# Start-up filler on a zeroed tile, one norm moved ahead of the next tile's first sums, and two column-tiled products made neighbours, in a fused linear-attention and FFN block

## The chip, the cores and the metric

The kernel runs on one core of one Trainium2 chip. The metric is device time in microseconds (us) of one execution; lower is better. The engines are TensorE (PE in the profile, with PEld for its weight loads), VectorE (DVE), ScalarE (ACT), GpSimd (POOL) and SyncE (SP), which issues most loads. A profile gives times from the first instruction of the span, and the measured time was 1.4 to 1.5 us longer than the span (225.25 against 223.8 in the profiled execution of the kernel before). The pitch is the time from the start of one matmul to the start of the next. In profile lines psT is the memory (PSUM) that matmul results go to.

## The reference

```python
x  = A_x                                   # 1 x 2048 x 640, bf16
xn = layernorm(x)                          # over 640 features
q, k, v = split(xn @ wqkv)                 # 32 heads of 20
phi(t)  = where(t > 0, t + 1, exp(t)) + 1e-6
kv  = einsum(phi(k), v);  z = sum_s phi(k) # per head
o   = (phi(q) @ kv) / (phi(q) . z + 1e-6)
s   = o @ wo
g   = silu(relu(xn @ w1) @ w2)             # w1: 640 x 1728, w2: 1728 x 640
out = x + s * g
```

The 1728 columns of w1 are 13 chunks of 128 and a half chunk of 64.

## The kernel before

Tokens are handled in 16 tiles of 128. For each tile VectorE takes the sums of two halves (`bn_stats`), aggregates them (`bn_aggr`) and normalises; GpSimd computes the inverse root of the variance (for tile 0 ScalarE and VectorE do). The step that normalises tile 1 is called norm 1, and so on. The normalised tile is transposed (for the first four tiles on TensorE, against an identity) and multiplied with the weights. The program gives each engine a list of operations with waits on semaphores, and the traces show the lists worked in order: in e7 below VectorE stands still for 1.00 us ahead of norm 1, for most of it with the next entry, tile 2's sums, ready (tile 2 landed at 6.14, norm 1 started at 6.88). These are the parts that the change touches:

```python
sc.op("POOL", lambda eng: eng.memset(ident[:], 0.0), ...)
sc.op("POOL", lambda eng: eng.affine_select(out=ident[:], ...), ...)        # L357
...
def warm(n):                                 # filler: keeps TensorE busy
    sc.group("PE", [(lambda eng: eng.matmul(ps[7][:, 0:P], lhsT=ident[:], rhs=ident[:], ...))
                    for _ in range(n)], R=[("ident",)], W=[("ps", 7)])      # L367
warm(33)
...
def LN_root_pool(t):                         # GpSimd: add eps (L391), then pow -0.5 (L393)
    ...
x_load(0); x_load(1); w_load(<first 3/5 of the key weights>)                # cut
x_load(2); x_load(3); w_load(<last 2/5 of the key weights>)                 # cut
...
LN_norm(0, late_loads)
transposes(0, 4)
warm(11)
xnT_copy(0, 4)
LN_stat(1, 1)
LN_aggr(1)
LN_root_pool(1)
LN_stat(2, 0)          # first sums of tile 2: wait for its load
LN_norm(1)             # waits for GpSimd's root of tile 1
K_mm(0, 0, range(0, KS))
transposes(1, 5)
...
def H_half(jp):        # half chunk of w1: 64 output columns, two token chunks side by side (L530)
    ...
def den():             # attention denominator: 32 output columns, four side by side (L616)
    ...
    # in the last token chunk: ... H_block(3,4), den(), H_block(3,5) ... H_block(3,12)
for jp in range(2):
    lastW1 = H_half(jp)
# then the sums over tokens, G = xn^T . phi(k) (L711)
```

## Time and profile before

| what | value |
|---|---|
| time, median of the first 3 executions | 225.07 us (224.62 to 225.43) |
| TensorE busy | 217.5 of 223.8 us |
| filler starts | 1.59 us |
| tile 2 landed | 7.08 us |
| transposes of tile 2 start | 10.10 us |
| steps between tilings in the stretch 99 to 113 us | 4 of 93 to 105 ns each |

The landing times in this document are the last of the 16 completion records of a load in the trace. First the page of the kernel before: part 1, and the engines' shares of the chain of part 4.

```profile
PE 217.5 (97%) x1447; PEld 134.8 (60%) x1457; DVE 102.8 (46%) x191; ACT 88.4 (39%) x146; POOL 45.2 (20%) x63
...
PE 94%; DMA 2%; DVE 2%; SPq 1%; issue 1%
```

TensorE fills the span, but the chain has 6% that is not TensorE, and it lies at the start and the end. The next lines are the chain that ended last, in order of time (start, length, what), of the kernel before.

```profile
2.20 4.89 DMA reg<-in_A_x_dram
7.08 0.02 issue
7.11 0.49 DVE stats L383
7.60 0.35 DVE reg L412
7.95 0.41 DVE stats L383
8.36 0.02 issue
8.38 0.21 DVE mv L387
8.59 0.76 DVE stats L383 x2
...
9.60 0.46 DVE reg L412
10.06 0.05 issue
10.10 0.45 PE psT L422 x5
```

The load that ends at 7.08 is tile 2. VectorE takes its first sums, then normalises tile 1 (L412 at 7.60; the chain counts a piece from the end of the one before it, its own start is 7.52), and so on to norm 2 and the transposes of tile 2 at 10.10. From there on it is TensorE, almost without a break, to the end. So the start is a chain of a load and VectorE.

The timeline of TensorE around the two tiled products of the kernel before (start, length from the first start to the last end, engine, line; idle time and its cause in brackets):

```profile
97.74 2.32 PE L517 MATMUL psT<-reg 128*128 128x512 bf16 x10
99.99 1.26 PE L616 MATMUL psT<-pqT,zmat 128*32 128x512 bf16 x20
101.41 8.58 PE L517 MATMUL psT<-reg 128*128 128x512 bf16 x39 [0.16 <-issue]
109.92 2.35 PE L530 MATMUL psT<-reg 128*64 128x512 bf16 x20
112.20 0.99 PE L711 MATMUL psT<-reg 128*128 128x320 bf16 x6
```

The weights' form (128\*128, 128\*32, 128\*64) shows the changes of tiling. The single records behind these lines give the steps: the last full-width start before 99.99 is at 99.68, 309 ns where neighbours are 216 apart. The 0.16 us before 101.41 is not idle time: that line has 39 matmul records and 40 weight loads, so the record of the first matmul is missing.

### The profile page before, as it was taken

How to read it: one execution, taken by the hardware profiler on the slowest of the kernel's cores; microseconds unless marked ns; L12 is line 12 of the kernel's file. 1: busy time of each engine (PE TensorE's matmuls, PEld its weight loads, DVE VectorE, ACT ScalarE, POOL GpSimd, SP SyncE). 2: the span in 40 equal slices, each digit the busy share in tenths (PEclk: the TensorE clock that was granted, in tenths of full speed). 3: DMA queues.
4: the chain of work that ended last, by engine and by line, in shares of the span. 5: the costliest groups of instructions: out<-in, count | busy, mean ns of one | idle time of the engine just before them, and what ended most of it. 6: DMA issues, size and time to landing. Idle time of an engine off the chain costs nothing.

```text
span 223.8 us, 3490 instructions
## 1 busy us (share of the span) xinstructions
PE 217.5 (97%) x1447; PEld 134.8 (60%) x1457; DVE 102.8 (46%) x191; ACT 88.4 (39%) x146; POOL 45.2 (20%) x63
## 2 busy tenths in 40 slices
PE   7999999999999999999999999999999999999993
PEld 6664555455554555444467778677767767776772
DVE  4669961796639772867000003940404041331472
ACT  4596966657665666654521111441021102102101
POOL 2426942322542245700000005000000000000001
PEclk9999999999999999999999999999999999999999
DMA  6999630012501150000899999900101010101030
GB/s 181 327 390 280 128 122 0 0 31 59 32 1 27 32 56 5 0 0 3 195 222 291 341 350 245 326 16 3 42 17 62 0 60 3 59 0 62 24 122 29
DMA packets 24333, 23.18 MB, mean 104 GB/s; under 512 B 9006, under 2 KB 23678, under 8 KB 24318
## 3 DMA queue, kind: packets, MB, share of 16 engines
q1 hardware_dynamic: 24174, 22.88, 37.2%
q8 instruction: 11, 0.18, 0.3%
q10 hardware_dynamic: 144, 0.08, 0.1%
q14 instruction: 4, 0.03, 0.0%
HBM read 15.75 MB, written 5.24 MB: 94 GB/s over the span
## 4 chain that ended last, share of the span: by engine, by line
PE 94%; DMA 2%; DVE 2%; SPq 1%; issue 1%
PE psT L778 26%; PE psT L517 25%; PE psT L711 10%; PE psT L494 10%; PE psT L439 9%; PE psT L817 8%; DMA reg<-in_A_x_dram 2%; PE psT L802 1%; PE psT L739 1%; PE psT L756 1%; PE psT L530 1%; DVE stats L383 1%; PE psT L724 1%; PE psT L616 1%; SPq L334 0%
## 5 line engine op out<-in xcount | busy, mean ns | idle before, releaser
L778 PE MATMUL psT<-reg,hT 128*128 128x320 bf16 x416 | 58.7, 299 | 0.3
L517 PE MATMUL psT<-reg 128*128 128x512 bf16 x252 | 56.8, 379 | 0.5 <-issue 0.2
L778 PEld LDWEIGHTS psT<-reg,hT 128*128 128x128 bf16 x416 | 40.3, 98 | 17.0 <-PE psT L756 1.6
L517 PEld LDWEIGHTS psT<-reg 128*128 128x128 bf16 x260 | 25.3, 98 | 29.2 <-ACT hT L521 0.4
L521 ACT ACTIVATE hT<-psT 128x512 bf16<-128x512 f32 x52 | 30.8, 600 | 17.7 <-PE psT L517 17.4
L774 ACT ACTIVATE reg<-psT 128x640 bf16<-128x640 f32 x16 | 10.8, 702 | 63.1 <-PE psT L778 34.8
L831 DVE TENSOR_TENSOR reg<-psT,reg 128x640 bf16<-128x640 f32 x14 | 11.5, 824 | 46.0 <-PE psT L817 46.0
L451 POOL TENSOR_TENSOR zacc<-zacc,reg 128x640 f32<-128x640 f32 x16 | 22.6, 1411 | 20.7 <-DVE reg L470 20.5
L439 PE MATMUL psT<-reg 128*128 128x320 bf16 x160 | 24.5, 299 | 0.0
L494 PE MATMUL psT<-reg 128*128 128x512 bf16 x98 | 21.8, 379 | 0.1
L711 PE MATMUL psT<-reg 128*128 128x320 bf16 x160 | 21.9, 299 | 0.0
L439 PEld LDWEIGHTS psT<-reg 128*128 128x128 bf16 x160 | 15.4, 98 | 7.8
L817 PE MATMUL psT<-reg,pqT 128*128 128x320 bf16 x140 | 20.0, 299 | 0.0
L711 PEld LDWEIGHTS psT<-reg 128*128 128x128 bf16 x160 | 15.6, 98 | 6.4 <-issue 0.4
L807 POOL TENSOR_TENSOR reg<-reg 128x320 bf16<-128x320 bf16 x1 | 0.8, 789 | 82.9 <-DVE reg L805 82.9
L817 PEld LDWEIGHTS psT<-reg,pqT 128*128 128x128 bf16 x140 | 13.7, 98 | 5.3
L727 DVE TENSOR_TENSOR reg<-psT,mh 120x120 bf16<-120x120 f32 (+1 forms) x6 | 1.5, 268 | 32.7 <-PE psT L724 32.6
L494 PEld LDWEIGHTS psT<-reg 128*128 128x128 bf16 x100 | 9.8, 98 | 11.1
L383 DVE BATCH_NORM_STATS2 stats<-reg 128x6 f32<-128x320 bf16 x32 | 14.2, 479 | 4.3 <-DMA reg<-in_A_x_dram 4.3
L501 ACT ACTIVATE er<-psT 128x512 bf16<-128x512 f32 x20 | 12.3, 614 | 9.1 <-PE psT L494 3.5
L456 ACT ACTIVATE ek<-psT 128x640 bf16<-128x640 f32 x16 | 11.4, 710 | 8.5 <-PE psT L439 8.4
L468 DVE TENSOR_SCALAR ek<-ek 128x640 bf16<-128x640 bf16 x16 | 6.1, 381 | 17.2 <-ACT ek L456 17.2
(63 smaller groups left out, 162.7 us busy)
## 6 DMA issues: line engine op xcount, KB each, us to landing
reg<-in_A_x_dram SPq DMA_DIRECT2D x16, 160.0 KB, 5.5
rden_by_feature<-rden SPq DMA_DIRECT2D x4, 640.0 KB, 8.8
reg<-rden_by_feature SPq DMA_DIRECT2D x5, 512.0 KB, 11.0
reg<-in_A_x_dram SPq DMA_DIRECT2D x4, 640.0 KB, 10.1
reg<-in_B_w_dram SPq DMA_DIRECT2D x2, 1120.0 KB, 10.1
out_dram<-reg SPq DMA_DIRECT2D x14, 160.0 KB, 1.8
reg<-in_B_w_dram SPq DMA_DIRECT2D x1, 1040.0 KB, 10.0
reg<-in_B_w_dram SPq DMA_DIRECT2D x1, 960.0 KB, 14.8
```

Source lines behind the costliest of these rows:

```text
L383: sc.op("DVE", lambda eng: eng.bn_stats(stats[:, t, a, :], xin[:, t % XR, HN * a:HN * (a + 1)]), R=[("xin", t % XR)], W=[("stats", t, a)])
L439: fns.append(lambda eng, a=a, k=k: eng.matmul(ps[b + a][:, 0:HN], lhsT=xnT[:, k, tok(t)], rhs=wqk[:, k, D + HN * a:D + HN * (a + 1)], star ...
L451: sc.op("POOL", lambda eng: eng.tensor_tensor(out=zacc[:, :], in0=zacc[:, :], in1=pk[:, t, :], op=ALU.add), R=[("zacc",), ("pk", t)], W=[( ...
L456: sc.op("ACT", lambda eng: eng.activation(out=e_.rearrange("p (a n) -> p a n", a=2), in_=ps2(b, HN), func=ACTF.Exp), R=[("ps", b), ("ps", ...
L494: sc.group("PE", [(lambda eng, k=k: eng.matmul(ps[b], lhsT=wqk[:, k, P * f:P * (f + 1)], rhs=xnT[:, k, schunk(j)], start=(k == 0), stop=(k ...
L501: sc.op("ACT", lambda eng: eng.activation(out=e_, in_=ps[b], func=ACTF.Exp), R=[("ps", b)], W=[("er_e", es)])
L517: a = sc.group("PE", [(lambda eng, k=k: eng.matmul(ps[b], lhsT=w1_sb[:, k, P * f:P * (f + 1)], rhs=xnT[:, k, schunk(j)], start=(k == 0), s ...
L521: sc.op("ACT", lambda eng: eng.activation(out=hT[:, f, schunk(j)], in_=ps[b], func=ACTF.Relu), R=[("ps", b)], W=[("hT", j, f)])
L711: fns.append(lambda eng, t=t, a=a: eng.matmul(ps[b + a][:, 0:HN], lhsT=xn[:, t, P * k:P * (k + 1)], rhs=pk[:, t, HN * a:HN * (a + 1)], sta ...
L778: fns = [(lambda eng, u=u, t=t, f=f, n=n: eng.matmul(ps[bs[n] + u][:, 0:HN], lhsT=hT[:, f, tok(t)], rhs=w2_sb[:, f, HN * n:HN * (n + 1)], ...
L817: sc.group("PE", [(lambda eng, c=c, a=a: eng.matmul(ps[b + a][:, 0:HN], lhsT=pqT[:, c, tok(t)], rhs=wf[:, c, HN * a:HN * (a + 1)], start=( ...
L831: sc.op("DVE", lambda eng: eng.tensor_tensor(out=tmpo[:, os_, lo:hi].rearrange(shp, a=na), in0=src, in1=g_sb[:, t, lo:hi].rearrange(shp, a ...
```

## The change

It makes three edits. The filler matmuls read a tile that VectorE zeroes, so they need not wait for GpSimd's identity; 38 in place of 33 keep their end where it was (near 5.1 us, starting from an estimated 1.05 in place of 1.59), at the slow pitch of 107 ns. Norm 1 goes ahead of the first sums of tile 2. The half-chunk products go directly behind the denominator product, so that the tiling changes three times in place of four (93 to 105 ns each in the kernel before).

```diff
+    fill = zmat[:, :, :].rearrange("p c h -> p (c h)")[:, 0:P]
+    sc.op("DVE", lambda eng: eng.memset(fill, 0.0), W=[("zmat",)])
+
     def warm(n):
-        sc.group("PE", [(lambda eng: eng.matmul(ps[7][:, 0:P], lhsT=ident[:], rhs=ident[:], start=True, stop=True))
-                        for _ in range(n)], R=[("ident",)], W=[("ps", 7)])
-    warm(33)
+        sc.group("PE", [(lambda eng: eng.matmul(ps[7][:, 0:P], lhsT=fill, rhs=fill, start=True, stop=True))
+                        for _ in range(n)], R=[("zmat",)], W=[("ps", 7)])
+    warm(38)
...
     LN_root_pool(1)
+    LN_norm(1)
     LN_stat(2, 0)
-    LN_norm(1)
...
                 if n == 9:
                     den()
+                    H_half(0)
+                    H_half(1)
...
-    for jp in range(2):
-        lastW1 = H_half(jp)
```

## The prediction

> **What bounds it now.** TensorE: busy 217.5 of 223.8 us (page, part 1), 94% of the chain that ended last; from 10.1 us the chain is TensorE nearly without a break. Before, it is the load of token tile 2 (landed 7.08), then VectorE (sums of tile 2 7.11, norm 1 7.52, sums 7.95, aggregation 8.38, sums of tile 3 8.59, norm 2 9.60), then the transposes of tile 2 at 10.10. A change earns only what it takes from that VectorE chain or from TensorE after 10.1.
>
> **1. Filler on a zeroed tile.** In the timeline the 33 fillers start at 1.59, released by GpSimd after the identity (memset 0.80, select 1.24 to 1.53). First work of engines starts at 0.80 and the identity's memset took 0.20, so I estimate the new start at 1.05. At the cold pitch (107 ns) 38 fillers end near 5.1, as 33 did: ahead of the first transposes (5.36, released by norm 0). VectorE idles until 3.16: its memset is free. What is bought is an earlier full clock: before, the pitch falls from 107 to 56 ns near 6.76. [...] If before 5.36, five transposes save 5 x 51 ns, but off the chain: tile 2 lands at 7.08 whatever TensorE does. Worth 0 to 0.3 us, 0.05 on average.
>
> **2. Norm 1 first.** Before, the sums of tile 2 waited for the load until 7.11 and norm 1 came behind, though its inverse root was ready at 6.92 (GpSimd, 6.35 + 0.57). After: norm 1 at 6.95, sums at 7.32 and 7.73, aggregation at 8.24 instead of 8.38. Norm 1 is 0.56 us earlier, but the chain gains only the idle time before 7.11: 0.14 us.
>
> **3. Products together.** In narrow timelines the last 128-column matmul starts at 99.68 and the den product at 99.99: 309 ns against the usual 216. The step back costs about the same (the "issue 0.16" after den is mostly a missing record: that line has 252 matmuls and 260 weight loads). The half-chunks pay 309 ns going in (109.61 to 109.92) and 312 going out (111.89 to 112.20). [...] the trace shows 93 to 100 ns each, four times. After: full to 32 columns, 32 to 64, 64 to full, so three[...]: 0.10 us gained[...]. All on the chain. PSUM banks: six in the ring, ScalarE evicts in 0.60 us while a block takes 1.08; no new wait. Gated loads still start behind the last up-projection product.
>
> **Sum.** 0.14 + 0.10 + 0.05 = 0.3 us of 225.07: 224.8 us, range 224.2 to 225.3. Run-to-run spread (0.8 us) exceeds the gain. Faster by over 2%: 0.01; within 2%: 0.98; slower: 0.01.
>
> **Right or wrong in the profile.** Filler start near 1.05; norm 1 near 6.95; transposes of tile 2 near 9.96; three steps of about 95 ns around 100 to 103 us and none at 112; span near 223.5.
>
> **What would make it wrong.** [...] tile 2 landing before 6.9, so that norm 1 delays its sums; GpSimd's root later than the load; a wait for a PSUM bank behind the half-chunks.

Passages that rest on something other than the traces of this case are cut out of the record, here and in one expectation (e4), and the cuts are marked. 0.14 (step 2) + 0.10 (step 3) + 0.05 (step 1) is 0.29, put as 0.3 us, which takes 225.07 to 224.8. In step 3 the alternative is 0.19 us if the step from 32 to 64 columns should cost nothing; it was not in the sum.

## The result, and the profile after

| | executions | median | range |
|---|---|---|---|
| before | 6 | 224.88 us | 224.62 to 225.43 |
| changed | 6 | 224.89 us | 224.84 to 224.95, and one of 465.64 |

The ratio of the fast executions is 0.9997 (95% interval 0.9983 to 1.0011). A ratio is the mean time of one kernel's fast runs over that of the other's of the same rounds, so it is not quite the ratio of the medians.

One execution, the profiled one, took 465.64 us. It is slow (over 1.5% above the fastest of the same kernel), and nothing below compares it with fast ones; a section of its own says what its trace shows. The profile of the changed kernel at the usual clock is that of its third run (e7 below; 223.4 us span). Its code has three lines more, so L383 of before is L386 here, L412 is L415, L616 is L619, L530 is L533 and L711 is L714. Its chain in order of time:

```profile
0.80 2.26 DMA reg<-in_A_x_dram
...
5.66 0.22 DVE mv L390
5.88 0.08 issue
5.96 0.24 POOL rsv L394
6.20 0.07 issue
6.27 0.58 POOL rsy L396
6.85 0.03 issue
6.88 0.45 DVE reg L415
7.32 0.80 DVE stats L386 x2
8.13 0.02 issue
8.15 0.21 DVE mv L390
8.36 0.76 DVE stats L386 x2
...
9.37 0.46 DVE reg L415
9.82 0.05 issue
9.87 0.45 PE psT L425 x5
```

The chain has changed its root. It no longer starts from tile 2 (landed at 6.14 in this execution, long before its sums at 7.32) but from tile 0, which landed at 3.06, and it runs through GpSimd: add at 5.96, power at 6.27, norm 1 at 6.88. VectorE, in order, stands still for 1.00 us in front of norm 1, with tile 2's sums ready to run for most of it.

The timeline of TensorE around the tiled products, same execution:

```profile
99.75 1.26 PE L619 MATMUL psT<-pqT,zmat 128*32 128x512 bf16 x20
100.95 2.35 PE L533 MATMUL psT<-reg 128*64 128x512 bf16 x20
103.45 8.58 PE L520 MATMUL psT<-reg 128*128 128x512 bf16 x39 [0.16 <-issue]
111.87 1.39 PE L714 MATMUL psT<-reg 128*128 128x320 bf16 x9
```

The products are neighbours. There are three steps: 309 ns going in, 309 between the last start of the 32-column and the first of the 64-column product, and 538 coming out, of which 216 are again a missing record (39 matmul records, 40 weight loads). At the sums over tokens (111.87) the step is an ordinary 215.

### The profile page after: what moved, and what is told of

It is laid out like the page before. It is cut to its first block, busy times and chain, and to the rows that moved or that the text cites. A ratio compares the mean times of both kernels' runs of the same rounds, so it can differ in the third digit from the quotient of the medians.

```text
span 464.2 us, 3501 instructions
## 1 busy us (share of the span) xinstructions
PE 457.0 (98%) x1452; PEld 204.5 (44%) x1462; DVE 99.4 (21%) x192; ACT 91.0 (20%) x146; POOL 44.6 (10%) x63
## 4 chain that ended last, share of the span: by engine, by line
PE 98%; issue 1%; DVE 0%
PE psT L781 26%; PE psT L520 26%; PE psT L714 10%; PE psT L442 10%; PE psT L497 10%; PE psT L820 9%; PE psT L370 1%; PE psT L742 1%; PE psT L805 1%; PE psT L759 1%; PE psT L533 1%; PE psT L727 1%; PE psT L425 1%; PE psT L619 1%; DVE reg L808 0%
## 5 line engine op out<-in xcount | busy, mean ns | idle before, releaser
L781 PE MATMUL psT<-reg,hT 128*128 128x320 bf16 x416 | 123.3, 502 | 0.3
L520 PE MATMUL psT<-reg 128*128 128x512 bf16 x252 | 120.5, 677 | 2.1 <-issue 2.1
L781 PEld LDWEIGHTS psT<-reg,hT 128*128 128x128 bf16 x416 | 61.2, 148 | 60.4 <-issue 17.8
L520 PEld LDWEIGHTS psT<-reg 128*128 128x128 bf16 x260 | 38.5, 149 | 78.8 <-issue 75.6
L442 PE MATMUL psT<-reg 128*128 128x320 bf16 x160 | 50.2, 504 | 0.0
L497 PE MATMUL psT<-reg 128*128 128x512 bf16 x98 | 46.6, 679 | 0.6 <-issue 0.6
L714 PE MATMUL psT<-reg 128*128 128x320 bf16 x160 | 46.9, 503 | 0.0
L820 PE MATMUL psT<-reg,pqT 128*128 128x320 bf16 x140 | 42.2, 503 | 0.0
L442 PEld LDWEIGHTS psT<-reg 128*128 128x128 bf16 x160 | 23.1, 146 | 26.2 <-issue 13.7
L714 PEld LDWEIGHTS psT<-reg 128*128 128x128 bf16 x160 | 23.9, 150 | 23.1 <-issue 7.5
L820 PEld LDWEIGHTS psT<-reg,pqT 128*128 128x128 bf16 x140 | 20.6, 147 | 20.3 <-issue 6.2
L497 PEld LDWEIGHTS psT<-reg 128*128 128x128 bf16 x100 | 15.2, 152 | 30.1 <-issue 29.4
L386 DVE BATCH_NORM_STATS2 stats<-reg 128x6 f32<-128x320 bf16 x32 | 14.1, 479 | 2.0 <-DMA reg<-in_A_x_dram 2.0
## 6 DMA issues: line engine op xcount, KB each, us to landing
reg<-rden_by_feature SPq DMA_DIRECT2D x5, 512.0 KB, 10.1
```

What stands on the lines that cost most here:

```text
L386: sc.op("DVE", lambda eng: eng.bn_stats(stats[:, t, a, :], xin[:, t % XR, HN * a:HN * (a + 1)]), R=[("xin", t % XR)], W=[("stats", t, a)])
L442: fns.append(lambda eng, a=a, k=k: eng.matmul(ps[b + a][:, 0:HN], lhsT=xnT[:, k, tok(t)], rhs=wqk[:, k, D + HN * a:D + HN * (a + 1)], star ...
L497: sc.group("PE", [(lambda eng, k=k: eng.matmul(ps[b], lhsT=wqk[:, k, P * f:P * (f + 1)], rhs=xnT[:, k, schunk(j)], start=(k == 0), stop=(k ...
L520: a = sc.group("PE", [(lambda eng, k=k: eng.matmul(ps[b], lhsT=w1_sb[:, k, P * f:P * (f + 1)], rhs=xnT[:, k, schunk(j)], start=(k == 0), s ...
L714: fns.append(lambda eng, t=t, a=a: eng.matmul(ps[b + a][:, 0:HN], lhsT=xn[:, t, P * k:P * (k + 1)], rhs=pk[:, t, HN * a:HN * (a + 1)], sta ...
L781: fns = [(lambda eng, u=u, t=t, f=f, n=n: eng.matmul(ps[bs[n] + u][:, 0:HN], lhsT=hT[:, f, tok(t)], rhs=w2_sb[:, f, HN * n:HN * (n + 1)], ...
```

## The experiments

Twelve kernels ran, in four calls. Each had six executions; the kernel before ran along eleven times in each call. Each call ran on another chip (10, 2, 7 and 0), so only times of one call are compared: the kernel before had means of 225.12, 225.05, 224.75 and 225.11 us in the four calls.

### Call 1: the changed kernel again, and each part alone

e1_again is the changed kernel without any edit.

> The changed kernel once more, to have a profile at the usual clock and more executions. Theory A (parts add up): the three gains of the prediction are there, span near 223.4 and the ratio to the kernel before about 0.9985 (0.3 us). Theory B (nothing is gained in the typical execution): the profiled execution of the kernel before, 225.25 us, was itself about 0.4 us slower than its typical one, ratio 0.9995 to 1.0005. On the execution of 465 us: theory C (it struck by chance, from outside the kernel) expects no such execution here, or as easily one of the kernel before; theory D (zero operands keep the clock from being released) expects it again in about one of six executions of this kernel and of e2, none in e3 and e4.

e2_filler_only: the diff's first part on the kernel before.

> Only the filler on the zeroed tile, 38 of them. Theory A: filler from about 1.05 us, full clock earlier than 6.76 us in some executions, 0 to 0.1 us gained, ratio 0.9996 to 1.0. Theory B: 0. Theory D of the 465 us execution: such executions appear here; theory C: they do not, more often than elsewhere.

e3_norm_only:

```diff
+    LN_norm(1)
     LN_stat(2, 0)
-    LN_norm(1)
```

> Only norm 1 ahead of the sums of tile 2. Theory A: the transposes of tile 2 about 0.14 us earlier (9.96 against 10.10) and the whole kernel 0.14 us shorter, ratio 0.9994. Theory B: the transposes of tile 2 come no earlier in relation to the first TensorE work after the loads, or the gain is given back before 20 us: ratio 1.0000.

e4_products_only: the diff's last two parts.

> Only the half-chunks moved behind the den product. Theory A: three steps between tilings of about 95 ns in place of four, 0.10 us gained, ratio 0.9996[...]. Theory B: the step from 64 columns to 128 costs more in this place than before the sums over tokens, or a wait for a PSUM bank appears behind it: gain 0.

| | median | range | ratio to before (95%) |
|---|---|---|---|
| before (11) | 225.17 | 224.58 to 225.75 | |
| e1 all | 224.99 | 224.91 to 225.12 | 0.9996 (0.9976 to 1.0016) |
| e2 filler | 225.19 | 225.00 to 225.48 | 1.0004 (0.9986 to 1.0023) |
| e3 norm | 225.01 | 224.99 to 225.13 | 0.9996 (0.9978 to 1.0014) |
| e4 products | 225.18 | 224.78 to 225.60 | 1.0004 (0.9984 to 1.0025) |

The ratios settle nothing, because the kernel before spreads over 1.2 us. The spread itself is the finding: the two kernels with norm 1 first lie within 0.14 and 0.21 us, the three without it spread over 0.5 to 1.2. The traces say why. This table has the landings of tile 0 and tile 2, the start of tile 2's transposes (T), the stretch from T to the start of the sums over tokens, and the time of the profiled execution less T. Three rows are from call 2, told of below.

| profile | tile 0 | tile 2 | T | T − tile 2 | T − tile 0 | T to sums over tokens | time − T |
|---|---|---|---|---|---|---|---|
| before | 3.14 | 7.08 | 10.10 | 3.02 | 6.97 | 102.10 | 215.15 |
| e2 filler | 3.11 | 6.99 | 10.01 | 3.02 | 6.90 | 102.10 | 215.12 |
| e4 products | 3.22 | 7.26 | 10.28 | 3.02 | 7.06 | 102.01 | 215.02 |
| e3 norm | 3.07 | 6.82 | 9.88 | 3.06 | 6.81 | 102.10 | 215.13 |
| e1 all | 3.16 | 6.60 | 9.97 | 3.37 | 6.81 | 102.00 | 214.99 |
| e5 norm (call 2) | 3.15 | 6.74 | 10.06 | 3.33 | 6.91 | 102.10 | 215.10 |
| e6 norm, products (call 2) | 3.08 | 6.77 | 9.88 | 3.11 | 6.80 | 102.00 | 215.04 |
| e7 all (call 2) | 3.06 | 6.14 | 9.87 | 3.73 | 6.81 | 102.00 | 215.04 |

In the old order T follows tile 2's landing by 3.02 us, each time. In the new order it follows tile 0's landing by 6.80 or 6.81 in four of five profiles, whatever tile 2 does. The fifth is e5 (6.91): there tile 1 landed at 4.35, where the other profiles of the table have 3.55 to 3.98, and VectorE came later to tile 1's sums, so that norm 1 started at 7.07. So norm 1 first does not take a fixed time off the chain; it exchanges a chain from tile 2 for one from tile 0. From these numbers, the exchange gains when tile 2 lands more than 6.81 − 3.02 = 3.79 us behind tile 0 (3.94 in the profile before, which gives 0.15) and earns nothing or loses when it lands sooner (3.44 in e1, 3.08 in e7). The losing side is worked out and not seen in this table: the three profiles of the old order have tile 2 at 3.88 to 4.04 behind tile 0, the five of the new order at 3.08 to 3.75.

The products gain 0.09 to 0.10 us in the stretch, wherever they are present. The filler changes neither the differences to T nor the stretch.

The last column shows that nothing else moves: it is 215.10 to 215.15 us without the products together and 214.99 to 215.04 with them. A difference in time beyond the products' 0.1 us is a difference in T. So e1's profiled execution took only 0.05 us less than e3's because its tile 0 landed 0.09 later, and e4's, with the products, took longer than e2's because its tile 2 landed 0.27 later. By the same sum, an estimate for an execution without a trace, the fastest of the kernel before in this call (224.58) had T near 9.46 and tile 2 near 6.44.

### Call 2: what adds up, and a shorter root

e5_norm_only_2 is e3 once more. e6_norm_products is e3 with the products. e7_again_2 is the changed kernel.

> Norm 1 first alone, once more, as the base of this call: its six executions lay within 0.14 us of each other, while those of the kernel before spread over 1.2 us, so differences of 0.1 us can be read against it. Theory A (with norm 1 first the start is bound by tile 0's load and GpSimd's inverse root of tile 1, no longer by tile 2's load): again within 0.2 us of each other, and the transposes of tile 2 start 6.81 us behind tile 0's landing. Theory B (the small spread was luck): a spread like that of the kernel before, about 1 us.

> Norm 1 first and the products together, filler as before. Theory A: 0.10 us faster than norm alone (three steps between tilings for four), the stretch from tile 2's transposes to the sums over tokens 102.0 us for 102.1. Theory B (the products' gain is given back in the time measured): equal to norm alone within 0.03 us.

> The changed kernel again, in the same call as norm alone and norm with products. Theory A (the early filler is worth nothing and costs nothing): equal to norm with products within 0.05 us, 0.10 faster than norm alone. Theory F (the early filler costs about 0.1 us, which is why the changed kernel and norm alone were equal, 225.01 and 225.02 on average, in the call before): 0.1 us slower than norm with products. On the slow execution: chance expects none here.

e8_root1_short is the changed kernel with one addition moved to VectorE:

```diff
     LN_aggr(1)
-    LN_root_pool(1)
+    sc.op("DVE", lambda eng: eng.tensor_scalar(out=rsv[:, 1:2], in0=mv[:, 1, 1:2], scalar1=EPS_LN, scalar2=None, op0=ALU.add), ...)
+    sc.op("POOL", lambda eng: eng.tensor_tensor(out=rsy[:, 1:2], in0=rsv[:, 1:2], in1=mhalf[:, :], op=ALU.pow), ...)
```

> The changed kernel with the addition of epsilon for tile 1 moved from GpSimd to VectorE, which shortens only the way to norm 1 (an addition of 0.23 us and the gap behind it on GpSimd against one of about 0.15 on VectorE). Theory A (norm 1's root binds the start): norm 1 about 0.15 us earlier behind tile 0's landing, and the kernel 0.10 to 0.17 us faster than the changed kernel, less where tile 2 lands late. Theory B (tile 2's load or TensorE's work binds): no change.

| | mean of 6 | range | ratio to before (95%) |
|---|---|---|---|
| before (11) | 225.05 | 224.64 to 225.65 | |
| e5 norm | 225.06 | 224.97 to 225.16 | 0.9999 (0.9984 to 1.0014) |
| e6 norm, products | 224.91 | 224.82 to 224.98 | 0.9993 (0.9979 to 1.0007) |
| e7 all | 224.90 | 224.85 to 224.94 | 0.9993 (0.9979 to 1.0006) |
| e8 all, short root | 224.82 | 224.65 to 224.98 | 0.9989 (0.9975 to 1.0003) |

The small spread of norm 1 first came again (0.19 us). On that quiet base the products show in the time: e6 is 0.15 us below e5, with non-overlapping ranges apart from a hundredth. Landings are part of these 0.15 us: the profiled executions differ by 0.24, of which 0.18 lie in T (e5's late tile 1) and 0.06 behind it. The expected 6.81 from tile 0's landing to T was missed in e5 (6.91). The early filler adds nothing and costs nothing: e7 and e6 differ by 0.01. In call 1 the changed kernel and norm alone had been equal (225.01 and 225.02 on average); call 2 does not repeat that, which speaks against the theory that the filler costs 0.1 us.

In e8 the timeline of VectorE shows the shortened way to norm 1:

```profile
5.57 0.21 DVE L390 BATCH_NORM_AGGREGATE mv<-stats 128x2 f32<-128x12 f32 x1
5.81 0.15 DVE L556 TENSOR_SCALAR rsv<-mv 128x1 f32<-128x1 f32 x1
6.63 0.45 DVE L415 TENSOR_SCALAR reg<-reg,mv,rsy 128x640 bf16<-128x640 bf16 x1 [0.67 <-POOL rsy L558]
6.99 0.88 DVE L386 BATCH_NORM_STATS2 stats<-reg 128x6 f32<-128x320 bf16 x2
```

From the aggregation to norm 1 it is 1.06 us; in e7 it was 1.22 (5.66 to 6.88). T came 6.66 us behind tile 0 in place of 6.81, so norm 1's root does bind the start of the changed kernel. In the time the mean fell by 0.08 us; two of the six executions (224.97 and 224.98) gained nothing. Tile 2 landing late in those two would explain it, but they have no trace.

### Call 3: the wait taken away by an earlier load, and no early filler

e9_tile2_early_old_order issues tile 2's load earlier and puts norm 1 back behind the first sums of tile 2:

```diff
+    x_load(2)
     w_load(wqk[:, 0:KS, D:2 * D], A_wqkv[0:P * KS, D:2 * D], ("wk", 0))
-    x_load(2)
     x_load(3)
...
-    LN_norm(1)
     LN_stat(2, 0)
+    LN_norm(1)
```

> The changed kernel with tile 2's load issued ahead of the first key weights and norm 1 put back behind the first sums of tile 2 (the order of the kernel before). It takes away the wait for tile 2's load by an earlier load. Theory A (the order of the kernel before lost only because tile 2 landed late; without that wait it is the better one, since its sums fill the time in which GpSimd computes norm 1's root): tile 2 lands before 5.5 us, the transposes of tile 2 start about 6.4 us behind tile 0's landing instead of 6.81, the kernel is 0.3 to 0.45 us faster than the changed kernel (about 224.5) and its executions lie within 0.2 us of each other instead of 1 us. Theory B (norm 1 first is better in itself): 0.1 us or more slower than the changed kernel. If the key weights, now later, bind the first products: transposes of tile 2 late behind TensorE, no gain.

e10_tile2_early_short_root has the early load, both sums of tile 2 ahead of norm 1, and e8's short root.

> As the run before, with both sums of tile 2 ahead of norm 1 and the epsilon of tile 1 added on VectorE. Theory A: norm 1 about 6.65 us, the transposes of tile 2 bound by TensorE's own work, not by VectorE; 0.1 to 0.3 us faster than the run before, 224.2 to 224.4, the fastest of all.

e11_hardly_any_filler is the changed kernel with `warm(1)` in place of `warm(38)`.

> The changed kernel with 1 early filler matmul instead of 38: an effect of the filler's timing, if there is one, many times enlarged. Theory A (TensorE is off the chain until tile 2's transposes, and the start of the filler matters only through the moment of the full clock): the full clock comes later, at 8 to 10 us instead of 4 to 7.5, the products before the transposes of tile 2 run at the cold pitch and delay them; 0.3 to 1.5 us slower. So the filler as such is needed, the 0.5 us of an earlier start are not. Rival (the filler is worth nothing at all): no change in time.

| | median | range | ratio to before (95%) |
|---|---|---|---|
| before (11) | 224.65 | 224.49 to 225.52 | |
| e9 | 224.83 | 224.58 to 225.06 | 1.0001 (0.9987 to 1.0016) |
| e10 | 224.47 | 224.32 to 225.43 | 0.9997 (0.9979 to 1.0016) |
| e11 | 225.61 | 224.97 to 226.27 | 1.0037 (1.0019 to 1.0054) |

The expected 0.3 us of e9 did not come in the time, nor the expected spread of 0.2 us (it was 0.48). On VectorE the wait was taken away: tile 2 landed at 4.76, its sums filled part of the time in front of norm 1, and the aggregation of tile 2 came at 7.80 in place of 8.15 in e7. But TensorE had a new wait. Timeline of TensorE, e9 then e10:

```profile
7.33 0.97 PE L442 MATMUL psT<-reg 128*128 128x320 bf16 x6 [0.95 <-DMA reg<-in_A_wqkv_dram]
8.15 0.44 PE L425 MATMUL psT<-ident,reg 128*128 128x128 bf16 x5
...
9.94 0.44 PE L425 MATMUL psT<-ident,reg 128*128 128x128 bf16 x5
```

```profile
7.87 0.97 PE L442 MATMUL psT<-reg 128*128 128x320 bf16 x6 [1.01 <-DMA reg<-in_A_wqkv_dram]
8.69 0.44 PE L425 MATMUL psT<-ident,reg 128*128 128x128 bf16 x5
...
10.48 0.44 PE L425 MATMUL psT<-ident,reg 128*128 128x128 bf16 x5
```

The key weights, now third in line behind the tiles, landed at 7.20 (e9) and 7.74 (e10), not at 5.70 to 6.85 as in the profiles with the old line of loads. The first products (L442) wait for them, and the transposes of tiles 1 and 2 stand behind in TensorE's order (in e9 norm 1 was done at 7.36, the transposes of tile 1 started at 8.15). In e9 norm 2 ran at 9.01, 0.36 earlier than in e7, and T was 9.94 all the same: with tile 2 early the old order is the faster one on VectorE, but this trace gains no time by it. In e10 tile 3 was late as well (8.15), but norm 2 was done at 9.61, and T, bound by TensorE, was 10.48. The wait moved from one load to another, the exception that the expectation of e9 had named. e10's executions spread over 1.1 us, as one would expect of a start bound by a late load (only the slowest of them has a trace); its median is the lowest, but two of its six executions took 225.12 and 225.43, and its mean (224.70) is that of the kernel before (224.75).

e11 shows that the early filler as such is needed. TensorE in e11:

```profile
1.05 0.29 PE L370 MATMUL psT<-zmat 128*128 128x128 bf16 x1 [1.05 <-DVE zmat L367]
...
7.00 1.81 PE L442 MATMUL psT<-reg 128*128 128x320 bf16 x6
8.60 0.74 PE L425 MATMUL psT<-ident,reg 128*128 128x128 bf16 x5
...
10.76 0.44 PE L425 MATMUL psT<-ident,reg 128*128 128x128 bf16 x5
```

The six products took 1.81 us at the slow pitch (0.97 to 0.99 at the full one), the full clock came at 9.67 (this and the other moments of the full clock are starts of the trace's clock record; in the kernel before it is 6.76, where the pitch falls from 107 to 56 ns), and T was at 10.76 although norm 2 had run at 9.40. The kernel lost 0.8 us against the kernel before. In the profiles of the kernels with the 33 or 38 fillers ahead of these products (call 4's apart), the full clock came between 3.8 and 7.4 us, early enough that TensorE did not set T, save in e9 and e10, where the weights did, and in e5 (7.43, the latest), where TensorE and norm 2 came to T together.

### Call 4: a second queue for the weights

e12_weights_second_queue is e10 with the two loads of key weights issued by ScalarE:

```diff
-    w_load(wqk[:, 0:KS, D:2 * D], A_wqkv[0:P * KS, D:2 * D], ("wk", 0))
+    w_load(wqk[:, 0:KS, D:2 * D], A_wqkv[0:P * KS, D:2 * D], ("wk", 0), E="ACT")
...
-    w_load(wqk[:, KS:C, D:2 * D], A_wqkv[P * KS:D, D:2 * D], ("wk", 1))
+    w_load(wqk[:, KS:C, D:2 * D], A_wqkv[P * KS:D, D:2 * D], ("wk", 1), E="ACT")
```

> As the run with tile 2 early and the short root (e10), with the two loads of key weights issued by ScalarE's queue in place of the common one, so that tiles 0 to 3 do not wait in line behind them nor they behind the tiles. An attempt at a version that beats both kernels. Theory A (the loads bind the start by the line in which they are issued): key weights land before 6.6 us and tile 2 before 5.5, the transposes of tile 2 start at about 9.3, 224.3 to 224.6 and ratio 0.997 to 0.999. Rival (the transfers themselves are the limit, so one load gets what another loses): tile 2 or the key weights land as late as in e10, and the time is that of the kernel before within 0.2 us.

It was slower: median 226.71 us (225.42 to 227.04) against 225.14, ratio 1.0063 (1.0041 to 1.0086). The key weights did land early (5.21 and 6.75), but tile 1 landed at 5.62 in place of 3.50 in e10 and tile 2 at 6.96 in place of 4.77. What one load gained the others lost, as the rival said (in e10 the weights landed at 7.74 and 8.99); whether they share a capacity, no run isolates. The rival's time, that of the kernel before within 0.2 us, was missed too: what follows was in neither theory. VectorE and then TensorE show what followed:

```profile
5.65 0.49 DVE L386 BATCH_NORM_STATS2 stats<-reg 128x6 f32<-128x320 bf16 x1 [1.02 <-DMA reg<-in_A_x_dram]
6.06 0.15 DVE L404 RECIPROCAL rsy<-rsv 128x1 f32<-128x1 f32 x1
6.24 0.45 DVE L415 TENSOR_SCALAR reg<-reg,mv,rsy 128x640 bf16<-128x640 bf16 x1
```

```profile
6.74 0.45 PE L425 MATMUL psT<-ident,reg 128*128 128x128 bf16 x5 [1.82 <-DVE reg L415]
...
7.99 1.78 PE L442 MATMUL psT<-reg 128*128 128x320 bf16 x6 [0.18 <-ACT reg L430]
9.56 0.74 PE L425 MATMUL psT<-ident,reg 128*128 128x128 bf16 x5
```

Tile 1's first sums stand ahead of tile 0's reciprocal in VectorE's order, so a late tile 1 delays tile 0. TensorE then idled for 1.82 us (to 6.74), and the full clock that had come at 4.38 was gone from 7.79 to 11.21, 3.42 us; the products of tile 0 took 1.78 us (0.97 in e9 and e10). That the loss came after the idle time is the order in this one trace; no run isolates its cause. Four of the six executions, the profiled one among them, have a mean clock of 0.992, and the fastest (225.42) has 0.998. The same in-order effect that the change exploits for tile 1 bites here for tile 0.

## The execution of 465 us

It is the one profiled as the changed kernel's first. Two lines of the page, the largest matmul group of that execution and the same group of the kernel before (line, count, then busy time and mean ns of one):

```profile
L781 PE MATMUL psT<-reg,hT 128*128 128x320 bf16 x416 | 123.3, 502 | 0.3
```

```profile
L778 PE MATMUL psT<-reg,hT 128*128 128x320 bf16 x416 | 58.7, 299 | 0.3
```

TensorE ran at about half its pace from beginning to end, and the trace has no clock record at all. The pace is not that of the slow pitch at the usual start, where starts are 106 or 107 ns apart: here the filler starts are 66, 56, 106, 56, 166, 55 and 166 ns apart, full pitch and pause in turn, from the first fifth of a microsecond on. So the slow pace was there before the filler could have done anything, and 450 us of dense ordinary products did not lift it. That speaks against the zero operands as its cause, but it is not proof: one of 54 executions of kernels with the zero filler was slow and none of 74 of kernels with the identity filler (50 of the kernel before, 24 of e3 to e6), which chance alone does easily (54 of 128 executions had the zero filler). It did not come again. Its cause stays open.

## Why the prediction was right or wrong

The predicted range (224.2 to 225.3) holds the measured 224.89, and "within 2%" was right. The point, 224.8, was near, but the gain of 0.3 us was too large. Against the kernel before the means are 0.11 us lower in call 1 and 0.15 in call 2; no interval leaves out a ratio of 1. The near hit of the point is luck in part: it was reckoned from 225.07, and the median of six executions of the kernel before was 224.88. In the profiles of the changed kernel (e1, e7) the signs that it named came: filler at 1.05, norm 1 at 6.97 and 6.88, T at 9.97 and 9.87, three steps and none at the sums over tokens, spans of 223.5 and 223.4.

- **What bounds it: right.** The chain of a load and VectorE up to 10.1 us, TensorE afterwards. The time from the sums over tokens to the last matmul was 107.76 or 107.77 us in all of the first five fast profiles.
- **Step 1, the filler (0.05 us): right that it is next to nothing.** The start at 1.05 was as estimated. In the five profiles with the identity filler of 33 the full clock came at 6.76, 7.12 (e3), 5.49 (e4), 7.43 (e5) and 6.74 (e6), in e1, e2, e7 and e8 with the early filler at 4.05, 6.79, 4.01 and 4.97. Earlier in some executions only, as e2's expectation has it, and off the chain, as the prediction said. The time from the filler's start to the full clock varies from execution to execution, from 2.78 us (e9) to 5.85 us (e5); what sets it is not shown.
- **Step 2, norm 1 first (0.14 us): the step that failed.** Its arithmetic for that one trace was right: norm 1 at 6.88 to 6.97 and the aggregation at 8.15 to 8.25, e5 (7.07, 8.34) apart. But the prediction took "the chain gains only the idle time before 7.11" from one profile as if tile 2 always landed at 7.08. That execution took 225.25 us, where the 44 executions of the kernel before in the four calls have a mean of 225.01 and a range of 224.49 to 225.75; tile 2's landing varies from one execution to the next (6.14 to 7.26 in the table). Measured alone, the step is worth 0.10 us in call 1 (225.02 against 225.12) and nothing in call 2 (225.06 against 225.05). It takes away the slow executions and the fast ones alike: where the two kernels ran together, the fastest execution of the kernel before (224.62, 224.58 and 224.64) is below the fastest of the changed one (224.84, 224.91 and 224.85). The prediction named this case ("tile 2 landing before 6.9, so that norm 1 delays its sums") and did not price it.
- **Step 3, products together (0.10 us): right.** The stretch fell from 102.10 to 102.00 or 102.01 us, and the step from 32 to 64 columns does cost as much as the others (309 ns for 216). In the time less T it is 0.10 us (means of 215.12 without, 215.02 with them). The plain times show it less cleanly: 0.15 us between e5 and e6, and e4 alone was 0.09 us above the kernel before (225.21 against 225.12), within their spreads of about 1 us. In the traces of the kernel before and of e7 a step is 93 to 106 ns over the ordinary 216 ns pitch at 512 columns; what happens in that time they do not show.

Where the gain went: 0.10 us of products arrived; of the start's 0.14 between nothing and 0.10 is left, not to be told from zero in this spread, because a wait for tile 2 was exchanged for a wait for GpSimd's root. e8 shows that this root is the new limit (0.15 us shorter, 0.15 us earlier). A version that beats both kernels clearly was not found: e8 has the lowest mean against the changed kernel of its own call (224.82 against 224.90), which is within the spread.

## What to carry to other kernels

Before costing a reorder by the idle time in one trace, ask what varies: here the load of tile 2 landed anywhere between 6.14 and 7.26 us, while T followed tile 0's landing by 6.80 or 6.81 in four of five profiles. Putting work that waits for an engine ahead of work that waits for a load steadied the time here (the fast executions of the changed kernel lie within 0.09 to 0.21 us of each other, where those of the kernel before spread over 0.8 to 1.2) rather than shortening it, since the engine, which works its list in order, now stands still for whichever comes first in it (VectorE for 1.00 us in e7). And moving a load forward in the shared line moved the wait to another load here (tile 2 landed at 4.76 in e9, but the key weights at 7.20 in place of 5.70 to 6.85): read all landings of the start before reordering one.
